# A one-element GpSimd copy behind every output scatter, and row scatters between the halves of a tile

## The chip, the cores and the metric

The kernel runs on one core of a Trainium2 chip. The metric is the device time of one execution in microseconds. The engines are named as in the profile: PE (TensorE; PEld is its weight load), DVE (VectorE), ACT (ScalarE), POOL (GpSimd) and SP (SyncE, which here issues DMAs). An indirect DMA is issued by POOL, which works out a destination for every row.

## The reference

A gated attention unit without softmax feeds a mixture of experts with a dense part. In numpy, cut to the core:

```python
scores = np.matmul(z, z.transpose(0, 2, 1)) / S        # z: 8 x 2816 x 64
x = (u * np.matmul(np.maximum(scores, 0) ** 2, v)).reshape(B * S, D)   # 22528 x 256
y_dense = np.maximum(x @ w1_dense, 0) @ w2_dense       # 256 -> 512 -> 256
expert_idx = np.argmax(x @ w_gate, axis=1)             # top 1 of 8
gate_w = softmax(x @ w_gate)[np.arange(N), expert_idx]
for e in range(E):
    mask = expert_idx == e
    y_moe[mask] = gate_w[mask, None] * (np.maximum(x[mask] @ w1[e], 0) @ w2[e])
out = y_dense + y_moe
```

The second stage is the one that the change touches: every token goes through the dense pair of weights and through one expert's pair.

## The kernel before, in words

**Attention stage** (up to about 580 us). Tiles of 128 tokens are computed for one batch after the other. A planner, with a cost for each piece of work and a time at which each engine is free, decides which engine does what and in which order; the order on PE, ACT, DVE and SP is written out by hand and not left to a scheduler. A finished tile lies in `pays` as 128 rows of 288 bf16: the 256 values of x, the gate weight and the token's number. When a group of up to 11 tiles is routed, every row gets a place in the DRAM table `xs`, which has a region for each expert, and the tiles join the list `waiting`. `scatter` (L688) then sends one tile's rows there: DVE casts the places to integers (`pi`, L693), and POOL issues an indirect DMA (L695). There are 176 such **row scatters**. Most go out in the attention stage; those of the last groups are left over, and 12 of them go out in the expert stage.

**Expert stage** (from about 582 us). It has two kinds of tiles. The first NT1 = 70 tiles hold 256 tokens of one expert each; they are built from the groups routed first. The rest hold two halves of 128 tokens, each half with an expert of its own; 20 such tiles run, and 2 more only if a count asks for it (it doesn't here). So 90 tiles with two halves each make 180 **output scatters**. The sizes of the steps:

- `fetch` (L859): SP loads a tile's rows from `xs`, transposed, and the gate weights and token numbers (`me`), up to 9 tiles ahead.
- `expert` (L887): DVE copies one expert's weights from the table `wall` in SBUF to a ring of 8 buffers (the "wall copy", L895). Which expert it is, DVE reads from a register.
- `up` (L899): 16 matmuls into a PSUM tile `h_ps` (3 buffers), then ACT's relu into the ring `h` (L910). It runs twice a tile, for the dense weights and for the expert's.
- `half` (L922): for 128 tokens, `down` (L915) makes 4 matmuls with the dense weights and 4 with the expert's into one PSUM tile `yy` (2 buffers). ACT copies the dense part to SBUF (L930). DVE multiplies the expert's part by the gate weight and adds the dense part into `ys`, a ring of 9 buffers (L931). POOL issues the output scatter, an indirect DMA that writes the 128 rows to their tokens' places in `out` (L933). After it may come a **pause** (L918): a POOL copy of the scattered tile to a buffer `idle` that nobody reads (the profile calls that buffer zr).

In the profile the rings of h, x, w, yd and ys are all called `ring`, since they lie in one buffer.

**Order.** POOL's order in this stage is that of the program. `slot` (L954) interleaves three tiles: the dense `up` of tile s, the second half of tile s−2, the fetch of a later tile, the wall copy for tile s+1, the expert `up` of tile s, and the first half of tile s−1. Behind the slot, the main loop (L1105) runs the pieces of routing that are due, and in every fifth slot one left row scatter, with a pause of its own. Before the change a pause stands behind the output scatter of first halves alone, for tiles below NT1, and copies the full width: 256 f32 per partition, 144 behind a row scatter. The tail of 128-token halves has none.

Of the kernel before, what the change touches and what calls it, by code (L numbers as in the profile page):

```python
# [8 lines left out]
F32 = mybir.dt.float32  # L9
# [10 lines left out]
def kernel(  # L20
# [12 lines left out]
    nc = tc.nc  # L33
# [8 lines left out]
    G = 11  # L42
# [7 lines left out]
    NT1 = -(-(Q1 * G * P - E * (T2 - 1)) // T2)  # L50
# [5 lines left out]
    ROW = 288  # L56
# [44 lines left out]
    pays = const.tile([P, 2 * G, WIDE], BF, name="pays")  # L101
# [180 lines left out]
    def offer(ready, rank, ways, then=None):  # L282
        count[0] += 1
        todo.append((rank, count[0], ready, ways, then))
# [396 lines left out]
    def nodep(ins, mine, *groups_):  # L681
        ins = ins.ins if hasattr(ins, "ins") else ins
        for key in groups_:
            tc.declare_no_dep(ins, group=key, reason="rows of different tokens")
        for key in mine:
            tc.add_to_no_dep_group(key, ins)
# [146 lines left out]
    def rings():  # L833

        def buf():
            return aA.tile([P, nK, 4 * P], BF, name="ring", tag="A")[:].rearrange("p k c -> p (k c)")
        def cut(r, o, n, size):
            return [r[:, o + i * size:o + (i + 1) * size] for i in range(n)]

        one, two, three = buf(), buf(), buf()  # L840
        ring["w"] = cut(one, 0, 4, WD) + cut(three, 0, 4, WD)
        ring["x"] = cut(one, 4 * WD, 5, 2 * T2) + cut(three, 4 * WD, 5, 2 * T2)
        ring["h"] = [a.rearrange("p (f t) -> p f t", f=4) for a in cut(two, 0, 6, 4 * T2)]
        ring["yd"] = [a.bitcast(F32) for a in cut(two, 24 * T2, 3, 2 * D)]
        ring["ys"] = cut(two, 24 * T2 + 6 * D, 7, 2 * D)
        ring["ys"] += cut(one, 4 * WD + 10 * T2, 1, 2 * D) + cut(three, 4 * WD + 10 * T2, 1, 2 * D)
        ring["ys"] = [a.bitcast(F32) for a in ring["ys"]]
        ring["idle"] = [zpool.tile([P, nK, dq], BF, name="zr", bufs=1)[:]
                        .rearrange("p k d -> p (k d)").bitcast(F32)]
# [3 lines left out]
    def take(name):  # L853
        if not ring:
            rings()
        turn[name] = turn.get(name, -1) + 1
        return ring[name][turn[name] % len(ring[name])]

    def fetch(s):  # L859

        x = take("x")
        me = mx.tile([P, 2, 2], F32, name="me", bufs=16)
        if s < NT1:
            R = nc.values_load(Rt[0][0:1, s:s + 1], engines=[ET.SP], min_val=0,
                               max_val=XROWS - T2,
                               skip_runtime_bounds_check_because="made by the table")
            xT = x.rearrange("p (c h t) -> p h c t", c=2, h=2)
            rows = xs[bass.ds(R, T2), :]
            for ins in (
                    nc.sync.dma_start_transpose(out=x.rearrange("p (c t) -> p c t", c=2),  # L870
                                                in_=rows.bitcast(BF)[:, 0:D]),
                    nc.sync.dma_start(out=me[:], in_=rows[:, P:P + 2].rearrange("(j p) c -> p j c", p=P))):

                nodep(ins, ["fx"], "xs2")
            return xT, me
        xT = x.rearrange("p (h c t) -> p h c t", c=2, h=2)
        k = 2 * (s - NT1)
        Rs = nc.values_load_multi_w_load_instructions(
            Rt[1][0:1, k:k + 2], engines=[ET.SP], min_val=0, max_val=XROWS - P,
            skip_runtime_bounds_check_because="made by the table")[1]  # L880
        for j in range(2):
            rows = xs[bass.ds(Rs[j], P), :]
            nc.sync.dma_start_transpose(out=xT[:, j], in_=rows.bitcast(BF)[:, 0:D])
            nc.sync.dma_start(out=me[:, j, :], in_=rows[:, P:P + 2])
        return xT, me

    def expert(s):  # L887
        k = 2 * (s - NT1)
        cells = Et[0][0:1, s:s + 1] if s < NT1 else Et[1][0:1, k:k + 2]
        wes = []  # L890
        for e in nc.values_load_multi_w_load_instructions(
                cells, engines=[ET.DVE], min_val=0, max_val=(E - 1) * WD,
                skip_runtime_bounds_check_because="made by the table")[1]:
            we = take("w")
            nc.vector.tensor_copy(we, wall[:].rearrange("p e w -> p (e w)")[:, bass.ds(e, WD)])  # L895
            wes.append(we)
        return wes

    def up(xT, ws):  # L899

        h_ps = late["s"].tile([P, 4, 2, P], F32, name="h_ps", tag="s")
        n = 2 // len(ws)
        for i, w1 in enumerate(ws):
            hs = slice(i * n, (i + 1) * n)
            for f in range(4):
                for c in range(2):
                    nc.tensor.matmul(out=h_ps[:, f, hs, :], lhsT=w1(c, f), rhs=xT[:, hs, c, :],  # L907
                                     start=(c == 0), stop=(c == 1))
        h = take("h")
        nc.scalar.activation(h, h_ps[:].rearrange("p f h t -> p f (h t)"), AF.Relu)  # L910
        return h

    def down(y, k, h, w2, j):
        for f in range(4):
            nc.tensor.matmul(out=y[:, k, :], lhsT=h[:, f, j * P:(j + 1) * P],  # L915
                             rhs=w2(f), start=(f == 0), stop=(f == 3))

    def pause(src):  # L918

        nc.gpsimd.tensor_copy(take("idle")[:, :src.shape[1]], src)  # L920

    def half(s, j):  # L922

        hd, he, we, me, ids = pend[s]
        we = we[j % len(we)]
        yd, ys = take("yd"), take("ys")
        y = late["y"].tile([P, 2, D], F32, name="yy", tag="y")
        down(y, 0, hd, lambda f: w2d[:, f, :], j)
        down(y, 1, he, lambda f: we[:, 2 * F + f * D:2 * F + (f + 1) * D], j)
        nc.scalar.copy(yd, y[:, 0, :])  # L930
        nc.vector.scalar_tensor_tensor(out=ys, in0=y[:, 1, :], scalar=me[:, j, 0:1],  # L931
                                       in1=yd, op0=ALU.mult, op1=ALU.add)
        ins = nc.gpsimd.indirect_dma_start(  # L933
            out=out, out_offset=bass.IndirectOffsetOnAxis(ap=ids[j], axis=0),
            in_=ys, in_offset=None, bounds_check=N - 1, oob_is_err=False)
        nodep(ins, ["out"], "out")
        if j == 0 and s < NT1:
            pause(ys)

    def tokens(s, me):  # L940
        mi = me[:].bitcast(I32)
        if s < NT1:
            return [mi[:, j, 1:2] for j in range(2)]
        ix = mx.tile([P, 2], I32, name="ix")
        nc.vector.tensor_tensor(out=ix[:], in0=mi[:, :, 1], in1=inv[:, 2 * (s - NT1):2 * (s - NT1) + 2],
                                op=ALU.bitwise_or)
        return [ix[:, j:j + 1] for j in range(2)]
# [6 lines left out]
    def slot(s, end):  # L954

        if s < end:
            xT, me = got.pop(s)
            we = wes.pop(s)
            hd = up(xT, [lambda c, f: w1d[:, c, f * P:(f + 1) * P]])
        if s - 2 in pend:  # L960
            half(s - 2, 1)
            del pend[s - 2]
        for _ in range(2):
            if fetched[0] < min(NT, s + 1 + AHEAD) and s < end:
                got[fetched[0]] = fetch(fetched[0])
                fetched[0] += 1
        if s + 1 < end:
            wes[s + 1] = expert(s + 1)
        if s == 1:
            half(0, 0)  # L970
        if s < end:
            he = up(xT, [lambda c, f, w=w: w[:, c * F + f * P:c * F + (f + 1) * P] for w in we])
            pend[s] = (hd, he, we, me, tokens(s, me))
        if s > 1 and s - 1 in pend:
            half(s - 1, 0)
# [31 lines left out]
    waiting = []  # L1007
    placed = set()

    def one_scatter(dve=True):  # L1010
        if not waiting:
            return
        g = waiting.pop(0)
        if dve:
            offer(now[0], 0, {"dve": (0.1, lambda eng: scatter(g))}, lambda t: placed.add(g))
        else:
            scatter(g)
            placed.add(g)
# [72 lines left out]
    for n, (b, i0, w) in enumerate(groups):  # L1091
        for i in range(i0, i0 + w, 2):
            g = b * nK + i
# [11 lines left out]
    for s in range(NT - MAYBE + 2):  # L1105
        assert s + AHEAD < NT1 or not waiting
        slot(s, NT - MAYBE)
        for fn in later.pop(nB + s, []):
            fn()
        if s % 5 == 1 and waiting:  # L1110
            g = waiting[0]
            one_scatter(dve=False)
            pause(pays[:, g % (2 * G), 0:ROW].bitcast(F32))
    assert not waiting
    assert not later
    n = nc.values_load(used[0:1, 0:1], min_val=0, max_val=NH,
# [35 lines left out]
```

## Time and profile before

| | us |
|---|---|
| median of 3 runs | 930.4 (929.56 to 930.82) |
| profiled execution | 937.3 |
| its span | 935.5 |
| PE busy in the span | 885.6 |
| DVE / ACT / POOL busy | 703.3 / 736.3 / 489.7 |
| mean granted clock | 0.987 |

The span runs from the first to the last instruction of the profiled execution; the time of that execution is 1.8 us longer, and it is 6.9 us longer than the median of the runs. In the answers of the trace that follow, a line such as L915 is a line of the kernel before; "out<-in" gives the names of the destination and the sources; after the bar stand the busy time of the group, the mean of one instruction in ns, the idle time of the engine just before them, and what ended most of it. In a view of one line's instructions, three numbers with slashes are the smallest, middle and largest duration in ns. The releaser that a view names is inferred from semaphore events, so the last one seen is named even where it had long been done.

### The profile page before, as it was taken

What the parts mean: (1) busy time and instruction counts of PE and PEld (TensorE: products, weight loads), DVE (VectorE), ACT (ScalarE), POOL (GpSimd) and SP (SyncE); (2) the same over time, 40 slices, a digit from 0 to 9 for tenths busy, and PEclk for the clock granted to TensorE, in tenths of its full rate; (3) what the DMA queues carried; (4) which work ended last, traced back from release to release, by engine and by line L of the source; (5) the groups of instructions that cost most, each with busy time, mean ns of one, the idle gap of its engine ahead of it and who ended that gap; (6) DMA issues with size and microseconds to landing.
All of it is one profiled execution on the core that took longest, in us unless ns stands there. A gap on an engine that the chain in (4) does not pass through costs nothing.

```text
span 935.5 us, 30562 instructions
## 1 busy us (share of the span) xinstructions
PE 885.6 (95%) x12256; PEld 763.3 (82%) x12256; DVE 703.3 (75%) x1319; ACT 736.3 (79%) x913; POOL 489.7 (52%) x525
## 2 busy tenths in 40 slices
PE   8999999999999999999999997999899998999996
PEld 5898888888888888888887775878787887888785
DVE  6999989999999999989997972656454444446553
ACT  7999989998989989989988770667666667677664
POOL 7203343335345344344446434577777877877455
PEclk9999999999999999999999988999999999999999
DMA  7994995996997999998998745565444444434332
GB/s 139 152 181 102 164 184 112 175 200 132 178 191 133 190 179 141 193 177 142 189 188 133 140 88 91 111 123 121 100 106 106 111 111 107 117 103 95 87 91 72
DMA packets 257871, 127.64 MB, mean 136 GB/s; under 512 B 225470, under 2 KB 232894, under 8 KB 257728
## 3 DMA queue, kind: packets, MB, share of 16 engines
q1 hardware_dynamic: 230112, 70.24, 45.2%
q0 software_dynamic: 27616, 55.44, 27.7%
q8 instruction: 96, 1.57, 0.7%
q14 instruction: 47, 0.39, 0.2%
HBM read 61.54 MB, written 37.16 MB: 105 GB/s over the span
## 4 chain that ended last, share of the span: by engine, by line
PE 64%; POOL 14%; issue 12%; DVE 4%; DMA 3%; ACT 1%; POOLq 1%; SPq 0%; another core or an unknown queue 0%; DVEq 0%; ACTq 0%
PE o L548 41%; PE s L383 10%; POOL out_dram L933 9%; PE h_ps L907 6%; PE yy L915 6%; POOL zr L920 2%; DMA xT<-pays 2%; PE lg L605 1%; DVE r L400 1%; POOL A L413 1%; DVE A L413 1%; DVE ring L931 1%; DMA out_dram<-ring,ix 1%; DVE ring L895 1%; DVE pays L577 1%
## 5 line engine op out<-in xcount | busy, mean ns | idle before, releaser
L548 PE MATMUL o<-vb,A 64*128 64x256 bf16 x7744 | 501.2, 272 | 8.9 <-issue 6.0
L548 PEld LDWEIGHTS <-A 64*128 64x128 bf16 x7744 | 412.2, 95 | 62.6 <-issue 11.8
L695 POOL DMA_INDIRECT xs<-pays,pi x176 | 199.3, 1133 | 276.6 <-DVE pi L693 220.6
L398 ACT ACTIVATE r<-s 128x1024 f32<-128x1024 f32 x279 | 275.3, 1014 | 38.5 <-PE s L383 29.0
L910 ACT ACTIVATE ring<-h_ps 128x1024 bf16<-128x1024 f32 x180 | 185.6, 1032 | 95.3 <-PE h_ps L907 40.5
L411 ACT ACTIVATE A<-r 128x1024 bf16<-128x1024 f32 x252 | 256.5, 1044 | 1.7 <-DVE r L400 1.3
L413 DVE TENSOR_TENSOR A<-r 128x1024 bf16<-128x1024 f32 x172 | 208.2, 1223 | 1.1 <-ACT r L398 0.2
L931 DVE SCALAR_TENSOR_TENSOR ring<-yy,me,ring 128x256 f32<-128x256 f32 x180 | 86.1, 482 | 151.6 <-ACT ring L930 84.2
L400 DVE TENSOR_SCALAR r<-s 128x1024 f32<-128x1024 f32 (+1 forms) x153 | 185.0, 1216 | 12.3 <-PE s L383 8.3
L933 POOL DMA_INDIRECT out_dram<-ring,me x140 | 146.2, 1044 | 66.5 <-DVE ring L931 32.5
L915 PEld LDWEIGHTS <-ring 128*128 128x128 bf16 x1440 | 139.8, 98 | 38.6 <-issue 22.8
L383 PE MATMUL s<-zT 64*128 64x512 bf16 (+1 forms) x944 | 162.7, 364 | 7.1 <-remote 2.8
L915 PE MATMUL yy<-w2d,ring 128*128 128x256 bf16 x720 | 107.9, 272 | 17.3 <-DVE ring L931 15.3
L915 PE MATMUL yy<-ring 128*128 128x256 bf16 x720 | 108.0, 273 | 0.0
L907 PE MATMUL h_ps<-ring,w1d 128*128 128x256 bf16 x720 | 94.0, 273 | 3.0 <-ACT ring L910 1.3
L907 PE MATMUL h_ps<-ring 128*128 128x256 bf16 (+1 forms) x880 | 95.3, 253 | 1.4 <-issue 0.8
L895 DVE COPY ring<-wall 128x2048 bf16 x110 | 85.0, 788 | 10.4 <-issue 5.9
L930 ACT COPY ring<-yy 128x256 f32<-128x256 f32 x180 | 68.1, 378 | 30.3 <-PE yy L915 14.5
L907 PEld LDWEIGHTS <-ring 128*128 128x128 bf16 x880 | 73.4, 98 | 11.8 <-DVE ring L895 3.3
L577 DVE TENSOR_TENSOR pays<-o,ut 128x512 bf16<-128x512 f32 x88 | 61.2, 696 | 26.3 <-PE o L548 16.1
L907 PEld LDWEIGHTS <-w1d 128*128 128x128 bf16 x720 | 69.9, 98 | 12.3 <-issue 4.3
L383 PEld LDWEIGHTS <-zT 64*128 64x128 bf16 x944 | 58.5, 95 | 26.1 <-issue 15.2
(120 smaller groups left out, 359.3 us busy)
## 6 DMA issues: line engine op xcount, KB each, us to landing
ut<-in_u_dram SPq DMA_DIRECT2D x88, 256.0 KB
vb<-in_v_dram POOLq DMA_DIRECT2D x16, 384.0 KB
vb<-in_v_dram POOLq DMA_DIRECT2D x16, 320.0 KB
wall<-in_moe_w_dram POOLq DMA_DIRECT2D x16, 256.0 KB
xs<-pays,pi POOLq DMA_INDIRECT x176
zr<-in_z_dram POOLq DMA_DIRECT2D x7, 352.0 KB
out_dram<-ring,me POOLq DMA_INDIRECT x140
A<-A SPq DMA_TRANSPOSE x128
```

The lines of the kernel that those rows point to most:

```text
L383: nc.tensor.matmul(out=s[:, h, y * c:(y + 1) * c], lhsT=zT[r, k + h, :], rhs=zT[r, i0:i0 + w, :], start=True, stop=True)
L398: nc.scalar.activation(r[:, :, :c], s[:, :, :c], AF.Relu, scale=1.0 / S)
L400: nc.vector.tensor_scalar(out=r[:, :, :c], in0=s[:, :, :c], scalar1=1.0 / S, scalar2=0.0, op0=ALU.mult, op1=ALU.max)
L411: nc.scalar.activation(a, r, AF.Square)
L413: (nc.gpsimd if eng == "pool" else nc.vector).tensor_mul(a, r, r)
L548: nc.tensor.matmul(out=o[:, j, 0:D], lhsT=A[n][r, k, c:c + P], rhs=v_of[b][r, k, :], start=(p == 0 and x == 0), stop=(p == 1 and x == nK - 1))
L695: ins = nc.gpsimd.indirect_dma_start(out=xs, out_offset=bass.IndirectOffsetOnAxis(ap=pi[:], axis=0), in_=pays[:, g % (2 * G), 0:ROW].bitca ...
L907: nc.tensor.matmul(out=h_ps[:, f, hs, :], lhsT=w1(c, f), rhs=xT[:, hs, c, :], start=(c == 0), stop=(c == 1))
L910: nc.scalar.activation(h, h_ps[:].rearrange("p f h t -> p f (h t)"), AF.Relu)
L915: nc.tensor.matmul(out=y[:, k, :], lhsT=h[:, f, j * P:(j + 1) * P], rhs=w2(f), start=(f == 0), stop=(f == 3))
L931: nc.vector.scalar_tensor_tensor(out=ys, in0=y[:, 1, :], scalar=me[:, j, 0:1], in1=yd, op0=ALU.mult, op1=ALU.add)
L933: ins = nc.gpsimd.indirect_dma_start(out=out, out_offset=bass.IndirectOffsetOnAxis(ap=ids[j], axis=0), in_=ys, in_offset=None, bounds_chec ...
```

## The change

Three edits: the pause copies one element per partition in place of the full width; it stands behind the output scatter of both halves (for tiles below NT1) in place of the first; and the left row scatter with its pause moves from the end of a slot, in slots 1, 6, 11 and so on, into the next slot, between the second half of tile s−2 and the fetch, so ahead of the wall copy, the expert `up` and the first half of tile s−1.

```diff
     def pause(src):
-        nc.gpsimd.tensor_copy(take("idle")[:, :src.shape[1]], src)
+        nc.gpsimd.tensor_copy(take("idle")[:, :1], src[:, :1])
...
     def half(s, j):
...
-        if j == 0 and s < NT1:
+        if s < NT1:
             pause(ys)
...
     def slot(s, end):
...
         if s - 2 in pend:
             half(s - 2, 1)
             del pend[s - 2]
+        if s % 5 == 2 and waiting:
+            g = waiting[0]
+            one_scatter(dve=False)
+            pause(pays[:, g % (2 * G), 0:ROW].bitcast(F32))
...
     for s in range(NT - MAYBE + 2):
         slot(s, NT - MAYBE)
         for fn in later.pop(nB + s, []):
             fn()
-        if s % 5 == 1 and waiting:
-            g = waiting[0]
-            one_scatter(dve=False)
-            pause(pays[:, g % (2 * G), 0:ROW].bitcast(F32))
```

On PE, ACT and SP the order of the instructions stays the same. On POOL there are 70 more copies, and 12 row scatters stand one output scatter later than before: ahead of them now goes the second half's scatter of the older tile. On DVE the 12 casts to `pi` now stand behind the L931 of that second half and ahead of the wall copy, and some 65 more semaphore waits stand at L931, which writes a `ys` buffer that an earlier pause has read. Nothing changes in the tail from tile 70 on.

## The prediction

> **What bounds the kernel now.** I read the page's slices first: GpSimd is busiest in the expert stage. Then the busy times of three stretches: expert tiles while left row scatters still go out, expert tiles after them, and the tail of half tiles, which has no pause before or after the change. Columns: stretch, length, busy time (and instructions) of PE, PEld, DVE, ACT, POOL, granted clock, DMA share, GB/s.
>
> ```profile
> 590.00:805.00 215.00, 199.01 (x1797) 174.39 (x1796) 109.84 (x229) 141.99 (x222) 161.45 (x189) 1.00 0.48 111
> 805.00:855.00 50.00, 48.80 (x461) 43.40 (x459) 26.43 (x46) 35.41 (x56) 38.61 (x43) 1.00 0.43 106
> 855.00:935.50 80.50, 69.11 (x735) 58.73 (x732) 42.38 (x94) 47.17 (x77) 43.04 (x41) 0.97 0.35 84
> ```
>
> PE is busy 92.6%, 97.6% and 85.8%; the clock is full in the first two. PE is the bound, and any gain or loss must come out of its 16.0 us of idle time in the first stretch and 1.2 in the second. TensorE's groups of those three stretches say what that idle time waits for (the last column: idle just before, and what ended it):
>
> ```profile
> L915 PE MATMUL yy<-w2d,ring 128*128 128x256 bf16 x448 | 67.1, 272 | 14.5 <-DVE ring L931 12.8 <-DVE pi L693 1.0 <-issue 0.3
> ...
> L915 PE MATMUL yy<-w2d,ring 128*128 128x256 bf16 x112 | 16.8, 272 | 1.2 <-DVE ring L931 1.2
> ...
> L915 PE MATMUL yy<-w2d,ring 128*128 128x256 bf16 x155 | 23.3, 272 | 1.6 <-DVE ring L931 1.3
> ```
>
> At 8 such matmuls a tile these are 56, 14 and 19.4 tiles. Nearly all idle time stands before the first matmul into a yy buffer, which waits until L931 has read the last content. L931 waits for ACT's L930, and ACT waits for PE. ACT's waits in the same stretches (total us, times, longest):
>
> ```profile
> ACT ring L910 <- PE yy L915: 26.2, 17, 2.6
> ACT ring L910 <- PE h_ps L907: 18.1, 37, 1.2
> ACT ring L930 <- PE h_ps L907: 10.8, 11, 1.4
> ACT ring L930 <- PE yy L915: 6.0, 9, 1.7
> ...
> ACT ring L910 <- PE yy L915: 5.7, 4, 1.7
> ACT ring L910 <- PE h_ps L907: 4.9, 10, 1.9
> ACT ring L930 <- PE yy L915: 2.4, 4, 1.3
> ACT ring L930 <- PE h_ps L907: 1.2, 1, 1.2
> ...
> ACT ring L910 <- PE h_ps L907: 17.4, 15, 2.9
> ACT ring L930 <- PE yy L915: 6.0, 7, 1.6
> ACT ring L910 <- PE yy L915: 2.7, 3, 1.7
> ACT ring L930 <- PE h_ps L907: 1.1, 1, 1.1
> ```
>
> Such a wait looks impossible: ACT waits for a PE that is done. The timeline at one of them (start, duration, then the instruction; idle time in brackets):
>
> ```profile
> 656.89 1.04 PE L907 MATMUL h_ps<-ring,w1d 128*128 128x256 bf16 x8
> 657.16 0.41 POOL L920 COPY zr<-ring 128x256 f32<-128x256 f32 x1
> ...
> 657.74 0.98 POOL L933 DMA_INDIRECT out_dram<-ring,me  x1 [0.17 <-issue]
> ...
> 657.86 0.37 ACT L930 COPY ring<-yy 128x256 f32<-128x256 f32 x1 [0.61 <-PE yy L915]
> ...
> 659.03 0.99 POOL L933 DMA_INDIRECT out_dram<-ring,me  x1 [0.30 <-DVE ring L931]
> ...
> 660.02 0.41 POOL L920 COPY zr<-ring 128x256 f32<-128x256 f32 x1
> ...
> 660.80 1.02 ACT L910 ACTIVATE ring<-h_ps 128x1024 bf16<-128x1024 f32 x1 [2.58 <-PE yy L915]
> ...
> 662.18 0.48 DVE L931 SCALAR_TENSOR_TENSOR ring<-yy,me,ring 128x256 f32<-128x256 f32 x1 [3.00 <-issue]
> ...
> 662.72 0.60 PE L915 MATMUL yy<-w2d,ring 128*128 128x256 bf16 x4 [1.29 <-DVE ring L931]
> ```
>
> The h_ps that L910 at 660.80 reads was complete at 656.89 + 1.04 = 657.93, and ACT was free at 658.23. L910 starts 2.58 us later, after two scatters in a row (657.74, 659.03), and PE loses 1.29 us. The opposite case:
>
> ```profile
> 697.71 1.24 POOL L933 DMA_INDIRECT out_dram<-ring,me  x1 [0.17 <-issue]
> ...
> 698.55 1.04 PE L907 MATMUL h_ps<-ring 128*128 128x256 bf16 x8
> ...
> 699.63 1.02 ACT L910 ACTIVATE ring<-h_ps 128x1024 bf16<-128x1024 f32 x1 [0.46 <-PE h_ps L907]
> ...
> 700.44 1.01 POOL L933 DMA_INDIRECT out_dram<-ring,me  x1 [1.49 <-DVE ring L931]
> ```
>
> Here h_ps ends at 699.59, with 1.9 us since the last scatter's start, and ACT starts 0.04 us later. My reading, inferred from such places: while GpSimd works on an indirect DMA, and shortly after, word of PE's finished groups reaches ACT late. Scatters at 1.29 us run together into one long block; a pause behind a scatter spreads them. So bounding PE is, in the end, how POOL's scatters are spaced.
>
> **The change, part by part.** *A: the pause becomes one element.* With a full pause the next scatter starts 657.74 − 656.18 = 1.56 us after the last (0.98 + 0.41 + 0.17, taking the scatter before 657.16 at 0.98). With none it is 0.98 + 0.30 = 1.29. A one-element copy isn't in the trace; bounds:
>
> ```profile
> L920 POOL COPY zr<-ring x70: 405/428/940, 588.8 to 853.7; 128x256 f32<-128x256 f32 x70
> L920 POOL COPY zr<-pays x12: 308/317/784, 589.3 to 804.3; 128x144 f32<-128x144 f32 x12
> ...
> L215 POOL IOTA pj<- 128x1 int32 x1 | 0.1, 129 | 0.0
> ```
>
> From below the 0.13 us of the IOTA over one element; from above the line through 308 ns at 144 and 405 at 256 elements, 0.87 ns an element, so 308 − 143 × 0.87 = 0.18. The pauses start where the scatter ends (660.02), so the new spacing is 0.98 + 0.13 to 0.18 + 0.17 = 1.28 to 1.33, that is, the spacing with no pause. I take 1.33 (the line is of this very copy). So 70 spreading pauses go, and none that spreads comes.
>
> Its price from the stretch without pauses, the tail: ACT's late time is 27.2 us over 19.4 tiles = 1.40 a tile, against 14.2 over 14 = 1.01 in the stretch with pauses and no row scatters. (The tail's tiles also differ in having two wall copies; there is no nearer row.) Over 70 tiles, 0.39 × 70 = 27.2 us of ACT. What share reaches PE: in the first stretch 14.5 of 61.1 us (0.24), in the second 1.2 of 14.2 (0.085). That gives +6.4 or +2.3; from below, PE's own rows give 1.6/19.4 − 1.2/14 = −0.003 a tile, nothing. All 27.2 would need every late microsecond to reach PE, and no stretch shows a share above 0.24, so that is left out. I take +6.4, since 56 of the 70 tiles are in the stretch with the 0.24.
>
> *B: the row scatter moves into the slot.* Twelve row scatters leave the end of a slot (behind half 0 and its pause) for the place between half 1's scatter and half 0's.
>
> ```profile
> L695 POOL DMA_INDIRECT xs<-pays,pi x12 | 12.8, 1070 | 2.5 <-issue 1.8 <-DVE pi L693 0.7
> ...
> L693 DVE CAST pi<-pos x12: 136/144/149, 589.9 to 800.8; 128x1 int32<-128x1 f32 x12
> ```
>
> What they cost now: PE's idle time per tile without them is 1.2/14 = 0.086; 56 × 0.086 = 4.8; the other 14.5 − 4.8 = 9.7 us belong to 12 row scatters, 0.81 each. One occupies POOL for 1.07 + 0.32 + 0.17 = 1.56 us now and 1.07 + 0.18 + 0.17 = 1.42 afterwards at the full gap, or 1.33 at the short one: 9 to 15% less. I take 15% of 9.7, −1.4. Bounds: −9.7 if the place between the halves makes it free, and +9.7 if it makes three contiguous scatters of two and doubles its price. Queues it is moved past: on POOL it goes ahead of half 0's scatter, which leaves 1.3 us later, and nobody waits for that landing but the ring of nine ys buffers. On DVE the 0.14 us cast goes ahead of the wall copy, in an engine idle for 105 of 215 us; if PE waited for that wall copy it would cost 12 × 0.14 = 1.7. On SP nothing of its own moves; the transposes keep their order.
>
> *C: 70 more copies and DVE's waits on POOL.* POOL has 53 us idle in the first stretch and the pauses fall from 70 × 0.43 + 12 × 0.32 = 33.9 us to 152 × 0.18 = 27.4: nothing. Each L931 now also waits for a pause that read its ys buffer nine halves ago. The queue's rows:
>
> ```profile
> L931 DVEq EVENT_SEMAPHORE  x136: 21/50/3858, 590.3 to 853.9; - x136
> ...
>   POOL zr L920: 5.2, 4
> ```
>
> About 65 more such instructions by the 50 ns median are 3.3 us in DVE's idle time; if they stood bare on PE's path, at 0.24, +0.8. Behind a late one would stand the wall copy and the next L931, and PE behind those. The 5.2 us put down to POOL are the same late ACT: the pause in question was over many scatters before. Zero.
>
> *Sum:* +6.4 − 1.4 + 0 = +5.0 us on the profiled execution's 937.3 (span 935.5, 1.8 around it), which becomes 942.3. That execution is 6.9 above the median of the runs, 930.4, so the difference is carried over to that: 935.4.
>
> **The rivals.** *R1, faster: the row scatter fits between the halves.* A tile is 48.8/14 = 3.49 us of PE, so halves end about 1.75 apart; a row scatter of 1.33 in that gap replaces one that had half 0's full pause before it and its own behind it. Then all of B's 9.7 goes, A costs the low +2.3, and the time is 923.0. For it: PE's idle time per tile is threefold where row scatters go out (0.26 against 0.086). Against it: the place at the end of a slot is also between two halves. It decides if idle time before L915 falls below 8 us in the first stretch.
>
> *R2, faster: short copies stay out of DVE's way.*
>
> ```profile
> L895 DVE COPY ring<-wall x73: 683/793/1164, 590.3 to 854.2; 128x2048 bf16 x73
> ...
> L895 DVE COPY ring<-wall 128x2048 bf16 x56 | 45.7, 816 | 3.4 <-issue 2.4
> ```
>
> The wall copy takes 683 to 1164 ns, mean 816, the pause 405 to 940: the two stretch each other. With no such meeting a tile gains 0.13 us of DVE, 9.3 in 70 tiles; at 0.24 that is −2.2, bare −9.3, in the middle −5.8: 924.6 with A at nothing. Against it: DVE is idle half the time, and scatters stretch too (1.24 at 697.71), which no shorter copy changes. The Trainium skill, "SBUF — State Buffer", section "Who interferes with whom", names a lock here: such a DVE copy and a GpSimd instruction exclude each other for a whole instruction. By that rule the full pause costs DVE time and the sum would be −5.8 instead of +5.0; the trace agrees on the stretching, but its late places are ACT's.
>
> *R3, faster: a gap of any kind is enough.* If it is the mere presence of an instruction between two scatters that lets PE's word through, then 140 gaps instead of 70 take off another 0.39 a tile: −6.4 and −1.4, 922.6. For it: no row shows that a long pause spreads better than a short one. Against it: a spacing of 1.33 is the 1.29 of the scatters at 657.74 and 659.03, which let nothing through.
>
> *R4, clearly slower:* B at its upper end: half 1's scatter, the row's and half 0's run together as one block of 3 × 1.33 = 4 us, longer than a tile's 3.5, and each row scatter costs 1.6: 6.4 + 9.7 = +16.1, 946.5. For it: two in a row already cost 2.58 of ACT at 658. Against it: half 0's scatter must wait for its own L931, which opens a gap.
>
> *R5, no change:* lateness stays in ACT's slack, as at the share 0.085, and A's low end +2.3 is taken back by B: about 930.4.
>
> **How the numbers follow.** Forecast (slower, 935.4): 0.36, its own range 932 to 940 (A at either share, B up to a third of its upper end, +3.2). R4 0.15; R1 0.13; R2 0.09; R3 0.13; R5 0.14. Faster 0.13 + 0.09 + 0.13 = 0.35, same 0.14, slower 0.36 + 0.15 = 0.51, where 0.2% (1.9 us) is what a measurement of this kernel can tell from no change. The two sides both hold much, so the range reaches from B's bound with A at nothing, 930.4 − 9.7 = 920.7, to R4: 920 to 947.
>
> **What would show it.** A: pauses of 0.13 to 0.18 us, scatters 1.28 to 1.33 us apart where they crowd; ACT's four waits for PE above 1.2 us a tile between 805 and 855; wrong if scatters stand 1.5 apart or those waits fall. B: idle time before L915's first matmul per row scatter still near 0.8 us, 3 to 9 us behind each; near zero means R1, above 1.2 R4. C: POOL busy some 6 us less, L931 waiting for POOL no longer than now. R2: mean of the wall copy below 0.75 us, with ACT's waits unchanged. R3: ACT's waits for PE below 0.8 us a tile between 805 and 855 although scatters stand 1.33 apart; this is what would make the forecast wrong soonest.

## The result, and the profile after

The changed kernel takes 936.0 us, the kernel before 929.9 us (medians of 22 runs each); the ratio is 1.0082, with a 95% interval of 1.0060 to 1.0104, so 5.6 to 9.7 us slower. The ratio leaves out the slow executions, one of the changed kernel (1128 us, at a granted clock of 0.75) and, as the numbers come out, the four longest of the kernel before (938 to 942 us); with those four in, the means differ by 5.6 us. The forecast was 935.4. The profiled execution of the changed kernel took 940.2 us (span 938.3).

The size and the side came out; whether the reason did is another matter, and the profile gives the first warning. The stretches of the changed kernel, with the columns of the prediction's first fence:

```profile
590.00:805.00 215.00, 201.56 (x1815) 177.04 (x1813) 107.56 (x244) 145.33 (x228) 160.88 (x242) 0.99 0.48 112
805.00:855.00 50.00, 47.43 (x439) 42.02 (x438) 23.19 (x42) 33.73 (x53) 37.56 (x55) 1.00 0.40 102
855.00:938.00 83.00, 71.19 (x784) 63.55 (x781) 45.46 (x101) 50.10 (x81) 48.74 (x48) 0.99 0.35 89
```

TensorE's groups in the same stretches, and then ACT's waits for PE in them:

```profile
L915 PE MATMUL yy<-w2d,ring 128*128 128x256 bf16 x448 | 67.6, 274 | 13.4 <-DVE ring L931 12.8 <-issue 0.4
...
L915 PE MATMUL yy<-w2d,ring 128*128 128x256 bf16 x108 | 16.2, 272 | 2.6 <-DVE ring L931 2.5
...
L915 PE MATMUL yy<-w2d,ring 128*128 128x256 bf16 x164 | 24.6, 272 | 4.5 <-DVE ring L931 4.2
```

```profile
ACT ring L910 <- PE h_ps L907: 31.6, 58, 2.2
ACT ring L930 <- PE yy L915: 14.8, 13, 2.0
ACT ring L910 <- PE yy L915: 9.6, 9, 1.8
ACT ring L930 <- PE h_ps L907: 9.1, 9, 2.9
...
ACT ring L910 <- PE h_ps L907: 4.5, 9, 1.1
ACT ring L930 <- PE h_ps L907: 4.1, 4, 1.2
ACT ring L910 <- PE yy L915: 3.7, 3, 2.5
ACT ring L930 <- PE yy L915: 2.6, 2, 1.4
...
ACT ring L910 <- PE yy L915: 11.5, 7, 4.0
ACT ring L930 <- PE yy L915: 7.0, 7, 1.4
ACT ring L910 <- PE h_ps L907: 6.5, 10, 1.0
ACT ring L930 <- PE h_ps L907: 0.8, 1, 0.8
```

The idle time before the first matmul into yy is 13.4 + 2.6 = 16.0 us in the two stretches that the change touches, against 14.5 + 1.2 = 15.7 before: no difference. ACT's waits there are 65.1 + 14.9 = 80.0 us against 75.3; how little such waits say is shown with the second chip below. More idle time than before stands only in the tail (4.5 against 1.6), which the change leaves as it was. The span splits at the last matmul group of the attention stage; of the kernel before, and of the changed one (range of starts):

```profile
L548 PE MATMUL o<-vb,A x7744: 266/269/418, 10.8 to 581.6; 64*128 64x256 bf16 x199
```

```profile
L548 PE MATMUL o<-vb,A x7744: 266/269/418, 10.5 to 586.4; 64*128 64x256 bf16 x199
```

The attention stage, whose program is the same in both, ended 4.8 us later, and from there to the end the changed kernel took 351.9 us (938.3 − 586.4) against 353.9. So this pair of executions, each some us above its own median, doesn't contain the 6 to 10 us that the 22 runs show. They have to be looked for by experiment.

What the change was said to do to single places can be seen. Of the changed kernel: its pauses, its row scatters, and the timeline of one of its worst places.

```profile
L920 POOL COPY zr<-ring x140: 191/196/722, 593.5 to 859.9; 128x1 f32<-128x1 f32 x140
...
L695 POOL DMA_INDIRECT xs<-pays,pi x13: 976/980/1402, 587.5 to 808.2; - x13
```

```profile
634.85 0.98 POOL L933 DMA_INDIRECT out_dram<-ring,me  x1 [0.15 <-DVE ring L895]
...
636.19 1.22 POOL L695 DMA_INDIRECT xs<-pays,pi  x1 [0.16 <-issue]
636.27 0.60 PE L915 MATMUL yy<-w2d,ring 128*128 128x256 bf16 x4
...
636.71 0.60 PE L915 MATMUL yy<-ring 128*128 128x256 bf16 x4
...
637.18 1.02 ACT L910 ACTIVATE ring<-h_ps 128x1024 bf16<-128x1024 f32 x1 [1.17 <-PE h_ps L907]
...
637.76 0.98 POOL L933 DMA_INDIRECT out_dram<-ring,me  x1 [0.16 <-issue]
...
639.10 0.98 POOL L933 DMA_INDIRECT out_dram<-ring,me  x1 [0.16 <-issue]
...
641.09 0.37 ACT L930 COPY ring<-yy 128x256 f32<-128x256 f32 x1 [2.88 <-PE h_ps L907]
...
642.08 0.64 PE L915 MATMUL yy<-w2d,ring 128*128 128x256 bf16 x4 [2.16 <-DVE ring L931]
```

Four indirect DMAs start 1.34, 1.57 and 1.34 us apart. The yy that L930 copies is complete at 636.71 + 0.60 = 637.31, ACT is free at 638.20, and L930 starts at 641.09, 2 us after the last scatter's start; PE loses 2.16 us. (An `up` of a whole tile is 8 matmuls, as the x8 beside L907 in the timelines shows; only the expert `up` of a tile of two halves has 16.)

### The profile page after: what moved, and what is told of

Read it like the earlier page. It is cut to its first block, busy times and chain, and to the rows that moved or that the text cites. A ratio compares the mean times of both kernels' runs of the same rounds, so it can differ in the third digit from the quotient of the medians.

```text
span 938.3 us, 30697 instructions
## 1 busy us (share of the span) xinstructions
PE 880.3 (94%) x12256; PEld 764.1 (81%) x12256; DVE 696.6 (74%) x1319; ACT 737.1 (79%) x913; POOL 491.4 (52%) x595
## 3 DMA queue, kind: packets, MB, share of 16 engines
q8 instruction: 96, 1.57, 0.7%
## 4 chain that ended last, share of the span: by engine, by line
PE 58%; POOL 16%; issue 9%; DVE 6%; DMA 4%; ACT 2%; SPq 1%; POOLq 1%; another core or an unknown queue 1%; DVEq 0%; ACTq 0%
PE o L548 36%; POOL out_dram L933 13%; PE s L383 8%; PE h_ps L907 6%; PE yy L915 6%; DMA xT<-pays 3%; POOL zr L920 3%; DVE r L400 2%; DVE A L413 1%; PE lg L605 1%; ACT A L411 1%; DMA vb<-in_v_dram 1%; ACT r L398 1%; POOLq L933 1%
## 5 line engine op out<-in xcount | busy, mean ns | idle before, releaser
L910 ACT ACTIVATE ring<-h_ps 128x1024 bf16<-128x1024 f32 x180 | 185.4, 1031 | 82.9 <-PE h_ps L907 42.5
L931 DVE SCALAR_TENSOR_TENSOR ring<-yy,me,ring 128x256 f32<-128x256 f32 x180 | 86.7, 483 | 154.0 <-ACT ring L930 97.6
L933 POOL DMA_INDIRECT out_dram<-ring,me x140 | 146.1, 1044 | 66.0 <-DVE ring L931 38.0
L915 PEld LDWEIGHTS <-ring 128*128 128x128 bf16 x1440 | 140.4, 98 | 41.6 <-issue 25.5
L383 PE MATMUL s<-zT 64*128 64x512 bf16 (+1 forms) x944 | 160.8, 360 | 8.3 <-remote 4.7
L915 PE MATMUL yy<-w2d,ring 128*128 128x256 bf16 x720 | 108.4, 273 | 20.5 <-DVE ring L931 19.6
L915 PE MATMUL yy<-ring 128*128 128x256 bf16 x720 | 108.5, 273 | 0.0
L930 ACT COPY ring<-yy 128x256 f32<-128x256 f32 x180 | 68.0, 378 | 39.3 <-PE yy L915 24.4
L907 PE MATMUL h_ps<-ring,w1d 128*128 128x256 bf16 x720 | 94.2, 274 | 0.8 <-DVE pays L577 0.8
L907 PE MATMUL h_ps<-ring 128*128 128x256 bf16 (+1 forms) x880 | 94.4, 253 | 0.5 <-issue 0.5
L895 DVE COPY ring<-wall 128x2048 bf16 x110 | 77.0, 715 | 11.5 <-issue 6.3
L907 PEld LDWEIGHTS <-ring 128*128 128x128 bf16 x880 | 74.2, 98 | 8.3 <-issue 1.0
L383 PEld LDWEIGHTS <-zT 64*128 64x128 bf16 x944 | 58.0, 94 | 25.8 <-issue 15.1
L907 PEld LDWEIGHTS <-w1d 128*128 128x128 bf16 x720 | 70.4, 98 | 9.6 <-issue 1.0
```

Source lines behind the costliest of these rows:

```text
L383: nc.tensor.matmul(out=s[:, h, y * c:(y + 1) * c], lhsT=zT[r, k + h, :], rhs=zT[r, i0:i0 + w, :], start=True, stop=True)
L933: ins = nc.gpsimd.indirect_dma_start(out=out, out_offset=bass.IndirectOffsetOnAxis(ap=ids[j], axis=0), in_=ys, in_offset=None, bounds_chec ...
```

## The experiments

Each group of runs went to one chip, with runs of the kernel before beside it. On all of these chips the kernel before takes 890 to 894 us, not 930, and that turned out to be the main finding.

**The two halves of the change, and two doses of the pause (first chip).** Short pauses behind both halves, row scatters where they were:

```diff
-        nc.gpsimd.tensor_copy(take("idle")[:, :src.shape[1]], src)
+        nc.gpsimd.tensor_copy(take("idle")[:, :1], src[:, :1])
...
-        if j == 0 and s < NT1:
+        if s < NT1:
```

> Half of the change alone: one-element pauses behind both halves, row scatters still at the end of a slot. Theory A (a pause works by its length, and a one-element pause spreads nothing): all of the loss and a little more, +6 to +9 us over the kernel before. Rival B (the place of the row scatter makes the loss): within 2 us of the kernel before. Rival R3 (any gap is enough, so the place must have cost what was measured): 5 to 7 us faster than before.

The row scatters moved, pauses as before:

```diff
         if s - 2 in pend:
             half(s - 2, 1)
             del pend[s - 2]
+        if s % 5 == 2 and waiting:
+            g = waiting[0]
+            one_scatter(dve=False)
+            pause(pays[:, g % (2 * G), 0:ROW].bitcast(F32))
...
-        if s % 5 == 1 and waiting:
-            g = waiting[0]
-            one_scatter(dve=False)
-            pause(pays[:, g % (2 * G), 0:ROW].bitcast(F32))
```

> The other half alone: row scatters between the halves, pauses as before (full width, behind first halves). Theory A: 0 to 2 us faster than before. Rival B: the measured +6 to +9 us. Rival R1: 7 to 10 us faster.

No pauses:

```diff
-        if j == 0 and s < NT1:
-            pause(ys)
...
             one_scatter(dve=False)
-            pause(pays[:, g % (2 * G), 0:ROW].bitcast(F32))
```

> No pause at all, row scatters at the end of a slot. Theory A: the same as one-element pauses behind both halves, within 3 us of that run, so 5 to 10 us slower than before. If short pauses do something after all (either way), this run and the one with short pauses differ by over 4 us. If pauses of any kind are worth nothing here: within 2 us of before.

Full-width pauses behind both halves:

```diff
-        if j == 0 and s < NT1:
+        if s < NT1:
```

> Full-width pauses behind both halves, row scatters at the end of a slot. Theory A (length spreads): another 70 spreading pauses, 3 to 6 us faster than before. Rival: POOL's load is what hurts, 140 pauses of 0.43 us bring it to 3.1 us of a 3.5 us tile: 3 us slower or more. No matter: within 2 us.

Measured against the kernel before (median 891.4): short pauses 0.9993 (0.9942 to 1.0043), row scatters moved 0.9970 (0.9938 to 1.0002), no pauses 0.9989 (0.9952 to 1.0026), full pauses behind both halves 1.0086 (1.0051 to 1.0121). On this chip neither half of the change costs anything that can be measured, and theory A's +6 us for losing the pauses is absent, even with no pause at all; the 3 to 6 us that it expected of full pauses behind both halves came out as a loss of 4.5 to 10.8. The stretch 590 to 805 without pauses, and with full pauses behind both halves, and in a third fence what DVE and PE wait for in the latter from 560 to 890:

```profile
590.00:805.00 215.00, 215.00 (x1972) 192.70 (x1970) 111.95 (x231) 158.42 (x247) 146.28 (x135) 1.00 0.52 121
```

```profile
590.00:805.00 215.00, 211.29 (x1920) 186.75 (x1918) 114.36 (x225) 155.19 (x240) 192.50 (x251) 1.00 0.48 113
```

```profile
...
DVE ring L931 <- DMA out_dram<-ring,me: 42.8, 30, 3.1
DVE ring L931 <- POOL zr L920: 24.1, 27, 3.0
...
PE h_ps L907 <- DMA ring<-xs: 3.4, 3, 1.5
PE yy L915 <- DVE ring L931: 2.5, 6, 0.8
```

Without pauses PE has no idle time at all. With 140 full pauses POOL is busy 192.5 of 215 us (90%), L931 waits for ys buffers whose pause or landing is outstanding, and PE waits before yy and for a tile's rows from `xs`. So the rival that POOL's load hurts is in keeping with this run, and with no other; which of these waits makes the loss isn't settled (PE's idle time in the stretch is 3.7 us of it).

**The change itself, and three of the runs again (second chip).**

> The changed kernel itself, once more. On the chip of the runs before (891 us, PE busy without a gap from 590 to 805 in three of the four traces) word of PE's groups was not late. If this chip is of that kind, theory A' (the change costs time only where PE's word is late) expects 0 to 3 us of difference from the kernel before; the rival (the cost has nothing to do with lateness) the 6 to 9 us that were measured first. If PE's word is late here (some 930 us), both expect 5 to 10 us slower.

> One-element pauses behind both halves, row scatters at the end of a slot. Where PE's word is late: theory A 6 to 9 us slower than before; rival B (the place of the row scatter) within 2 us. Where it isn't: within 2 us, as on the last chip (0.9993).

> Row scatters between the halves, pauses as before. Where PE's word is late: theory A 0 to 2 us faster; rival B 6 to 9 us slower; R1 7 to 10 us faster. Where it isn't: 0 to 3 us faster, as on the last chip (0.997).

> No pause at all. Where PE's word is late: theory A as with one-element pauses behind both halves (within 3 us of that run) and 5 to 10 us slower than before; if the pause is worth nothing, within 2 us of before. Where it isn't late: within 2 us of before, as on the last chip (0.9989), with PE busy throughout.

Against 890.5: the change 0.9982 (0.9941 to 1.0024), short pauses 0.9999 (0.9952 to 1.0047), row scatters moved 0.9948 (0.9911 to 0.9985), no pauses 0.9951 (0.9909 to 0.9993). The same program that was 5.6 to 9.7 us slower in the first measurement is between 5 us faster and 2 us slower here. Its stretch, and a place of it with four indirect DMAs in a row, to be held beside the place at 634 to 642 above:

```profile
590.00:805.00 215.00, 215.00 (x1972) 192.72 (x1970) 112.26 (x231) 158.44 (x247) 175.40 (x268) 1.00 0.49 120
```

```profile
640.62 0.98 POOL L695 DMA_INDIRECT xs<-pays,pi  x1 [0.16 <-DVE ring L931]
640.97 1.04 PE L907 MATMUL h_ps<-ring 128*128 128x256 bf16 x8
...
641.95 1.03 POOL L933 DMA_INDIRECT out_dram<-ring,me  x1 [0.16 <-issue]
642.05 1.02 ACT L910 ACTIVATE ring<-h_ps 128x1024 bf16<-128x1024 f32 x1 [0.46 <-issue]
...
643.35 0.98 POOL L933 DMA_INDIRECT out_dram<-ring,me  x1 [0.16 <-issue]
...
644.69 0.98 POOL L933 DMA_INDIRECT out_dram<-ring,me  x1 [0.16 <-issue]
```

The starts are 1.33, 1.40 and 1.34 us apart, as crowded as at 634. Here h_ps is complete at 640.97 + 1.04 = 642.01 and ACT starts at 642.05, 0.04 us later, 0.1 us after a scatter's start. PE's word (its semaphore signal) is never late in this trace: from 590 to 855 no L910 or L930 starts more than 0.04 us after both its matmul group and ACT's instruction before it have ended. Yet ACT, busy 158.44 of 215 us, waits for PE often:

```profile
ACT ring L910 <- PE h_ps L907: 50.1, 109, 0.5
```

So the sum of ACT's waits is no measure of late word. Lateness counted from the end of the matmul group or of ACT's instruction before, whichever is later (delays over 0.1 us summed over L910 and L930 from 590 to 855), is 62.8 us in the kernel before at 930 us, 57.1 in the changed one, and nothing here.

Moving the row scatters alone came out 0.3% and 0.5% faster on the two chips, having no pauses 0.1% and 0.5%, both just clear of no change on the second; their traces give it no place in the expert stage: PE is busy 215.00 of 215 us in all four. What moves from one execution to the next is the attention stage, which nobody edited. In the changed kernel's trace here it ended so:

```profile
L548 PE MATMUL o<-vb,A x7744: 266/269/417, 10.8 to 556.4; 64*128 64x256 bf16 x199
```

From there to the end are 883.9 − 556.4 = 327.5 us. In the traces of short pauses, of moved row scatters and of no pauses on both chips that rest is 326.0 to 327.5 us, while the attention stage ends anywhere from 559.1 to 566.4. Only full pauses behind both halves have a longer rest, 336.9. So the differences of up to 0.5% aren't explained. The kernel before has no trace at 890 us to compare with, but these seven agree within 1.5 us in the stage that was edited.

**The length of the pause alone.**

```diff
-        nc.gpsimd.tensor_copy(take("idle")[:, :src.shape[1]], src)
+        nc.gpsimd.tensor_copy(take("idle")[:, :1], src[:, :1])
```

> The length of the pause alone: one element in place of the full width, still behind first halves only, row scatters at the end of a slot. On a chip where word of PE's groups is late (some 930 us before): theory A 5 to 9 us slower; rival R3 (any gap is enough) within 2 us; rival R2 (short copies stay out of DVE's way) 2 to 9 us faster. On a chip where it isn't late (some 890 us before): within 2 us, with PE busy without a gap in the expert stage, and the wall copy's mean falls from about 0.80 us to 0.70 with no gain from it.

0.9996 (0.9963 to 1.0029), beside 890.4. The wall copy in the run with moved row scatters and full pauses, and in this one with short pauses:

```profile
L895 DVE COPY ring<-wall 128x2048 bf16 x61 | 44.8, 734 | 2.1 <-issue 0.4
```

```profile
L895 DVE COPY ring<-wall 128x2048 bf16 x61 | 42.4, 695 | 1.0
```

The wall copy gets 39 ns shorter, as R2 said, and nothing comes of it: PE is busy 215.00 of 215 us in both.

**ACT made late on purpose (third chip).** The late word itself couldn't be called up, so its effect was put in by hand: small copies on ACT ahead of the dense relu in 12 slots, with the kernel before, with the changed kernel, and with fifteen copies in place of ten (`slow` is a 128 x 64 tile of its own).

```diff
             we = wes.pop(s)
+            if s % 5 == 2 and s < 60:
+                for _ in range(10):
+                    nc.scalar.copy(slow[:], slow[:])
             hd = up(xT, [lambda c, f: w1d[:, c, f * P:(f + 1) * P]])
```

> The kernel before, with ACT made late on purpose: in slots 2, 7, 12 ... 57 (12 of them) ten small copies of 64 columns, about 2.3 us together, stand ahead of the dense relu, where the traces of the 930 us runs show ACT waiting for word of PE. Theory A'' (on those runs the cost is ACT's lateness beyond the slack that two yy buffers give; 2.58 us late cost PE 1.29 there): PE loses about 1 us at each, 9 to 15 us in all, before the first matmul into yy, with L931 as the releaser. Rival (lateness of ACT is absorbed, the idle time of PE has another cause): under 3 us in all, with PE busy as before.

> The changed kernel with the same ten copies in the same slots. If the pauses and the place of the row scatter act only through when PE's word gets through, the loss here is that of the kernel before with the copies, within 2 us. If the change also makes recovery from a late ACT slower (three scatters in a row on POOL behind each late place), this run is 4 to 8 us slower than that one.

> The kernel before with fifteen copies in place of ten, about 3.5 us at each place. Theory A'': what is beyond the slack goes to PE in full, so each place costs about 1.2 us more than with ten, 12 to 16 us more in all. Rival: as with ten, under 3 us in all.

Against 893.8: 1.0104 (1.0033 to 1.0175), 1.0107 (1.0046 to 1.0168) and 1.0327 (1.0260 to 1.0395). Copies (stretch 565 to 800) and TensorE's group (580 to 800) in the kernel before with ten copies, in the changed kernel with ten, and in the kernel before with fifteen (here L917 is what L915 is elsewhere, L933 is L931, and L963 are the copies):

```profile
L963 ACT COPY slow<-slow 128x64 bf16<-128x64 bf16 x120 | 29.4, 245 | 3.4
...
L917 PE MATMUL yy<-w2d,ring 128*128 128x256 bf16 x484 | 72.6, 272 | 5.7 <-DVE ring L933 5.7
```

```profile
L917 PE MATMUL yy<-w2d,ring 128*128 128x256 bf16 x484 | 72.6, 272 | 5.7 <-DVE pi L695 5.7
```

```profile
L963 ACT COPY slow<-slow 128x64 bf16<-128x64 bf16 x180 | 44.0, 245 | 5.3
...
L917 PE MATMUL yy<-w2d,ring 128*128 128x256 bf16 x452 | 67.8, 272 | 20.9 <-DVE ring L933 20.9
```

Ten copies hold ACT for (29.4 + 3.4)/12 = 2.73 us, and PE loses 5.7/11 = 0.52 at each of the 11 places in the stretch; fifteen hold it for (44.0 + 5.3)/12 = 4.11, and PE loses 20.9/11 = 1.90. So 1.38 more on ACT is 1.38 more on PE: up to some 2.2 us of lateness is absorbed here, and what is beyond goes to PE in full. The first dose cost half of the microsecond a place that was expected. At the two places of the 930 us traces less was absorbed, 2.58 − 1.29 = 1.29 us and 2.88 − 2.16 = 0.72; why isn't known. PE's idle time falls in front of the same matmul, with L931 or the cast behind it as the releaser, as in the 930 us traces. And the changed kernel loses what the kernel before loses, 5.7 us before yy; the intervals of the two runs alone would allow several us of difference, but in their traces the rest after the attention stage is 336.7 us in the kernel before and 336.1 in the changed one. Its crowded scatters don't slow the recovery.

## Why the prediction was right, and where it wasn't

**What bounds the kernel** held in its first half, as far as times can show it, and for the 930 us executions only. "While GpSimd works on an indirect DMA, and shortly after, word of PE's finished groups reaches ACT late": in the two 930 us traces, from 590 to 855 and where ACT stood free, L910 began 0.77 us (before, 17 times) and 0.47 us (changed, 15 times) after the end of its matmul group on average when that end came 0.4 to 0.8 us after an indirect DMA's start, and 0.04 us after it when the end came 1.6 us or more after one (8 and 16 times). In the changed kernel's 890 us trace it began 0.04 us after it at every distance. That lateness costs PE only beyond a slack, before yy, was shown by putting it in by hand. The second half, that the spacing of the scatters decides, was not borne out: from 590 to 855 the starts less than 1.4 us apart went from 30 to 50 with the change, and the lateness from 62.8 to 57.1 us; with 52 such starts on the second chip there was none.

**A, the term that carried the forecast, was not borne out, and that the time came out within a microsecond is, as far as the runs show, luck.** The pauses came at 0.196 us (0.13 to 0.18 expected) and crowded scatters at 1.34 (1.28 to 1.33 expected). The step that failed is "Over 70 tiles, 0.39 × 70 = 27.2 us of ACT": in the profiled pair ACT's four waits grew by 65.1 + 14.9 − 61.1 − 14.2 = 4.7 us in the two stretches, and between 805 and 855 from 14.2 to 14.9, where above 1.2 us a tile was to show it (14.9/13.5 = 1.10). PE's idle time before yy there grew by 0.3 us where A and B together put +5.0. Two things were wrong in it. It called ACT's waits for PE "late time", and most of a wait can be ordinary: 50.1 us of them stood where nothing was late. And the tail was the wrong stretch: in the changed kernel, with the same program, its waits were 25.8 us in 20.5 tiles (164/8), 1.26, where they had been 1.40. On chips without late word, taking pauses away or shortening them cost nothing in any of five runs.

**B is in keeping with the trace.** Row scatters were to keep their price, 3 to 9 us behind each: in the kernel before 10.6 of the 14.5 us in the first stretch stand there, in the changed one 9.6 of 13.4, and of the 2.6 in the second, 1.55 us at 813.95, behind the row scatter at 808.2 that now falls into it. R1 (below 8 us) is out. R4's block of contiguous scatters did form at 634 and cost 2.16, but the sum over the stretch didn't rise, so R4's +16.1 is out too.

**C** said that the copies cost nothing, and nothing in the runs speaks against that, but they were dearer than 0.18: copies that met a wall copy took up to 0.72 us, and POOL's busy time over the span went from 489.7 to 491.4, not 6 us down. The line of the page, and the wall copy of the changed kernel between 590 and 805:

```profile
PE 880.3 (94%) x12256; PEld 764.1 (81%) x12256; DVE 696.6 (74%) x1319; ACT 737.1 (79%) x913; POOL 491.4 (52%) x595
```

```profile
L895 DVE COPY ring<-wall 128x2048 bf16 x56 | 40.3, 719 | 3.9 <-issue 2.7
```

**R2**'s mechanism is real (the wall copy's mean fell from 816 to 719 ns in the first stretch of the 930 us pair) and moved no time where it was tried alone, at 890 us. The lock that the Trainium skill describes ("SBUF — State Buffer", "Who interferes with whom") agrees with these rows and with a one-element copy that lasted 0.72 us. **R3**, like R2, had the change faster, and at 930 us it was slower; at 890 us no word is late that a gap could let through. **R5**'s "no change" is what the chips of the experiments show, but not for R5's reason, since there is no lateness there to be absorbed.

**What stays open.** The 6.1 us between the medians was measured where PE's word is late, and none of the runs that take the change apart met that condition. Which half costs it there, and where in the span it lies, isn't settled: the one profiled pair has it in neither stretch that was edited, and the end of the attention stage alone moved by 10 us between executions at 890 us. That lateness is the condition for it is supported (no loss on the second chip, none of either half on the first), not shown.

## What to carry to other kernels

Before explaining a small difference, see whether one profiled pair contains it, and whether the kernel before takes the same time on the chip of the experiment; here 930 and 890 us were different regimes, with different bounds, and a loss was measured in one only. Before calling a wait late, look at when the thing waited for was done: an engine with time to spare waits all the time. A stretch that lacks the feature in question is a poor measure of its price when it differs in other ways too. A wait that ends late is worth only what lies beyond the slack behind it; measure that slack by putting in a delay of two sizes.

## What the hardware showed that was not expected

The delay between a finished matmul group and the engine waiting for it isn't fixed: 0.04 us with the same crowding of indirect DMAs on one chip, up to 2.9 us in the 930 us executions between 590 and 805, and the granted clock (0.99 to 1.00 in that stretch against 1.00) doesn't tell them apart. Without it the expert stage runs with PE busy 215.00 of 215 us, and from the end of the attention stage to the end the changed kernel takes 327.5 us, not 351.9. The other 30.0 us between the spans of these two executions lie in the attention stage (556.4 against 586.4); these runs don't tell how much of that is late word. Why those executions have it and the three chips of the experiments don't wasn't found.
